# Two attention layers with a dense layer after each: in the second attention stage, a block's averages are moved from the start of the block ahead of it to the middle of the one before that

## The chip, the cores and the metric

The kernel runs on one core of one Trainium2 chip. The metric is the device time of one execution in microseconds (us); the time of a kernel is the median of its runs. Five engines work side by side, each in the order of its own instructions, and wait for each other by semaphores: PE (TensorE, matrix products into PSUM), DVE (VectorE), ACT (ScalarE), POOL (GpSimd) and SP (SyncE, which here issues every DMA).

## The reference

All tensors are float32. There are 2048 rows of 640, 32 heads of 20, and 1536 hidden columns; A and B are applied in turn, twice, each to the row-normalized x and each added to x.

```python
def A(x):                       # linear attention with a learned feature map
    q, k, v = split(x @ wqkv)   # 32 heads of 20
    pq, pk = q @ w_phi, k @ w_phi            # per head
    phi_q = concat(softmax(pq), softmax(-pq))
    phi_k = concat(softmax(pk), softmax(-pk))
    kv, z = phi_k.T @ v, phi_k.sum(rows)     # over all 2048 rows
    o = (phi_q @ kv) / (phi_q @ z + 1e-6)
    return o @ wo
def B(x):                       # dense, Mish, dense
    h = x @ w1 + b1
    return (h * tanh(softplus(h))) @ w2
x = x + A(norm(x)); x = x + B(norm(x)); x = x + A(norm(x)); x = x + B(norm(x))
```

## The kernel before

Each layer has three stages. The first attention stage makes the features of all rows: keys and values go into one PSUM tile that sums `kv` and `z` over all rows, and the queries' features, turned, are spilled to DRAM tensors `e_d`, one for each block. The **second attention stage** (`attend_second`, L783) needs the finished `kv`: it loads the turned features again, multiplies them with `kv`, divides, turns the result, multiplies it with `wo` and adds it to x. The dense stage follows.

The rows are cut into NB = 8 blocks of 256, and a block into two tiles of 128 rows, t = 0 and 1. For each block the second stage has these steps:

- `load(b)` (L755): three DMAs that bring the turned features of block b from `e_d` (two big tiles and one small one).
- `average(b, t)` (L791): 22 small products (L801) of these features with `kvb`, 64 rows at a time, into the two banks of one PSUM tile named `mm`. They give numerators and denominators of the 32 heads. It returns a function that divides.
- `divide` (L808): on DVE, add 1e-6 to the denominators (L816, twice), reciprocal (L817), multiply (L820, twice), into a row tile `xn`.
- `Transposed(rows).all()` (L326): ten PE transpositions of the two divided row tiles, into three PSUM tiles named `one` (four, four and two transpositions). ACT copies the high part of each out (`xth`), and DVE subtracts it for the low part (`xtl`, L332). Products are made from high and low parts, three for each.
- `Rows.half(c, ps)` (L832): fifteen products of 128 x 320 (L416) with `wo` into one `one` tile; then DVE adds them to x (L840) and takes statistics for the next norm (L841). Of the two row tiles `r0` and `r1`, each has two halves: four halves a block, sixty products.

The PSUM tiles named `one` come from a pool of four buffers, those named `mm` from a pool of two; a new tile takes the buffer that was given out longest ago, and its first writer waits until the readers of the old tile have ended. A block takes seven `one` tiles in this order: r0 half 0, r0 half 1, r1 half 0, three for the transpositions, r1 half 1.

Within this stage the order on PE, DVE and SP is the order in which the code is written (`tc.manual_schedule`); ACT and POOL are ordered by a scheduler. `block(b)` (L848) begins with the averages of block b + 1 and their divisions; then come r0's halves, r1's first half, the transpositions of block b + 1, and r1's second half. Behind it stand the mean of r1 (L845), the statistics on POOL (L300, L301), the store of the block (L884), fetches and parts of weights for the dense stage, and the steps of `tail`, which end the features of the last two row tiles of the first stage: softmax sums (L452 to L464), the turn on DVE (L514) and their spills (L518). These are spread over blocks 0 to 3. The loads of block b + 3 are issued in the middle of block b. The averages of blocks 0 and 1 stand ahead of the loop.

Of the kernel before, what the change touches and what calls it, by code (L numbers as in the profile page):

```python
# [24 lines left out]
BT = 2  # L25
BLK = BT * P
NB = S // BLK
# [24 lines left out]
def kernel(  # L52
# [25 lines left out]
    def one_tile():  # L78
        return psum.tile([P, 512], F32, tag="one", name="one", bufs=4)
# [10 lines left out]
    def row_block(t, b):  # L90
        return t[b * BLK:(b + 1) * BLK, :].rearrange("(p t) d -> p t d", t=BT)
# [203 lines left out]
    def norm_scale(b, mvs, t0=0, later=False):  # L295

        n = len(mvs)
        ve = work.tile([P, BT], F32, tag="ve", name="ve", bufs=2)
        for t in range(n):
            nc.gpsimd.tensor_scalar(ve[:, t:t + 1], mvs[t][:, 1:2], LN_EPS, 1.0, op0=ALU.add, op1=ALU.mult)  # L300
        nc.gpsimd.tensor_tensor(stats[:, b, 0, t0:t0 + n], ve[:, :n], neg_half[:, :n], op=ALU.pow)  # L301

        def shifts():
            for t in range(n):
                nc.vector.tensor_scalar(stats[:, b, 1, t0 + t:t0 + t + 1], mvs[t][:, 0:1],
                                        stats[:, b, 0, t0 + t:t0 + t + 1], -1.0, op0=ALU.mult, op1=ALU.mult)
        if later:
            return shifts
        shifts()

    class Transposed:
# [25 lines left out]
        def all(self):  # L337
            while len(self.hs) < KD:
                self.step()
            return self  # L340
# [25 lines left out]
    def row_tile():  # L366
        return work.tile([P, D], F32, tag="xn", name="xn", bufs=4)
# [41 lines left out]
    def project_half(ps, xts, t, ws, col, c, ks=range(KD), w=HC, final=KD - 1, ns=(0, 1, 2), end=2):  # L409
        sl = slice(t * P, (t + 1) * P)  # L410
        cs = slice(col + c * w, col + (c + 1) * w)
        for k in ks:
            h, l, wh, wl = xts.hs[k], xts.ls[k], ws[k][0][:, cs], ws[k][1][:, cs]
            for n in ns:
                a, r = ((h, wh), (h, wl), (l, wh))[n]
                nc.tensor.matmul(ps[:, :w], a[:, sl], r, start=(k == 0 and n == 0),  # L416
                                 stop=(k == final and n == end))

    def halves():
        mm = mm_tile()  # L420
        return [mm[:, 0], mm[:, 1]]
# [46 lines left out]
    def fetch(x_src, b, xt=None):  # L468
        xt = x_tile() if xt is None else xt
        nc.sync.dma_start(xt, row_block(x_src, b))  # L470
        return xt
# [311 lines left out]
    def attend_second(x_src, x_dst, acc, fetches, makes, fetch_next, begin_next):  # L783
        kva, o_ws, loaded, rest, late = acc
        rows = {}
        div = [None]

        def tail(i):
            next(late[i], None)

        def average(b, t, po=None):  # L791

            phs = loaded[b]
            po = halves() if po is None else po
            for g in range(G):
                n = 120 if g < 10 else 80
                w = GW if g < 10 else 42
                c, j = divmod(g, 8)
                for q in range(2):
                    s0 = t * P + 64 * q  # L800
                    nc.tensor.matmul(  # L801
                        po[c][64 * q:64 * q + 64, GW * j:GW * j + w], phs[g][:n, s0:s0 + 64],
                        kvb[:n, g, :w], start=True, stop=True)
            if t == BT - 1:
                del loaded[b]
            return lambda: divide(b, po)

        def divide(b, po):  # L808

            o = row_tile()  # L810
            den = work.tile([P, H], F32, tag="r", name="den", bufs=2)
            pv = [po[c][:, :(DH + 1) * n].rearrange("p (h d) -> p h d", d=DH + 1)
                  for c, n in ((0, 24), (1, 8))]
            hh = (slice(0, 24), slice(24, H))
            for c in range(2):
                nc.vector.tensor_scalar_add(den[:, hh[c]], pv[c][:, :, DH], DEN_EPS)  # L816
            nc.vector.reciprocal(den, den)  # L817
            for c in range(2):
                n = hh[c].stop - hh[c].start
                ins = nc.vector.tensor_tensor(o.rearrange("p (h d) -> p h d", d=DH)[:, hh[c]], pv[c][:, :, :DH],  # L820
                                        den[:, hh[c]].unsqueeze(2).to_broadcast([P, n, DH]), op=ALU.mult)
                div[0] = ins.ins
            rows.setdefault(b, []).append(o)

        class Rows:


            def __init__(self, b, t, cur):
                self.b, self.t, self.xt, self.cur = b, t, xs[b], cur
                self.bn = work.tile([P, 2, 6], F32, tag="bn", name="bn", bufs=2)  # L830

            def half(self, c, ps):  # L832
                if self.b == self.t == c == 0:
                    for ks in ((0, 1), (2, 3), (4,)):
                        for ns in ((0, 1), (2,)):
                            project_half(ps, self.cur, 0, o_ws, 0, 0, ks, ns=ns)
                else:
                    project_half(ps, self.cur, self.t, o_ws, 0, c)
                part = self.xt[:, self.t, c * HC:(c + 1) * HC]
                nc.vector.tensor_tensor(part, ps[:, :HC], part, op=ALU.add)  # L840
                nc.vector.bn_stats(self.bn[:, c], part)  # L841

            def mean(self):
                mv = work.tile([P, 2], F32, tag="mv", name="mv", bufs=3)
                nc.vector.bn_aggr(mv, self.bn)  # L845
                return mv

        def block(b, cur, behind=()):  # L848

            if b == NB - 1:  # L850
                ahead[0].all()
            elif b:
                for t in range(BT):
                    average(b + 1, t)()
            r0, r1 = Rows(b, 0, cur), Rows(b, 1, cur)
            for d in behind[:1]:
                d()
            r0.half(0, one_tile())
            if b:
                tail(0)  # L860
                tail(1)
            for d in behind[1:]:
                d()
            if b + 1 < NB:
                xs[b + 1] = fetch(x_src, b + 1)
            if 0 < b and b + 3 < NB:
                loaded[b + 3] = load(b + 3)
            if b == NB - 3:
                fetch_next()
            r0.half(1, one_tile())  # L870
            mv0 = r0.mean()
            if left:
                left.pop()()
            if b == 1:
                tail(1)
            if b == NB - 2:
                ahead.append(begin_next())
            r1.half(0, one_tile())
            if b + 1 < NB:
                cur = Transposed(rows.pop(b + 1)).all()  # L880
            r1.half(1, one_tile())
            left.append(norm_scale(b, [mv0, r1.mean()], later=True))
            xt = xs.pop(b)
            nc.sync.dma_start(row_block(x_dst, b), xt)  # L884
            makes[b]()
            if b + 1 < NB:
                fetches[b + 1]()
            tail(0)
            for _ in range((0, 1, 1, 2)[b] if b < 4 else 0):
                tail(1)  # L890
            return cur

        ahead, left = [], []
        E = mybir.EngineType
        with tc.manual_schedule(engines={E.PE, E.SP, E.DVE}):
            kv = finish_kv(kva)
            next(rest)
            next(kv)
            xs = {0: fetch(x_src, 0)}
            fetches[0]()  # L900
            next(rest)
            next(kv)
            next(rest)
            tail(0)
            tail(0)
            first = [average(0, t) for t in range(BT)]
            for d in first:
                d()
            with tc.issue_after(div[0]):
                loaded[2] = load(2)  # L910
            tail(0)
            singles = [one_tile(), one_tile()]
            behind = [average(1, 0, singles), average(1, 1)]
            loaded[3] = load(3)
            cur = Transposed(rows.pop(0))
            pair = halves()
            cur.step()
            cur.step(pair[0])
            cur.step(singles[1][:, BLK:])
            for b in range(NB):  # L920
                cur = block(b, cur, () if b else behind)
            left.pop()()
            assert all(next(g, 0) == 0 for g in late)
        return ahead[0]
# [248 lines left out]
```

## Time and profile before

| what | value |
|---|---|
| median of 3 runs | 1355.46 us (1354.35 to 1355.51) |
| the profiled execution | 1355.98 us, of which the span is 1354.1 us |
| granted TensorE clock | 1.0 |
| busy in the span: PE, DVE, ACT, POOL | 1348.3, 1069.7, 584.6, 468.9 us |
| second attention stage, layer 0, averages of block 2 to those of block 7 | 264.71 to 328.86 us |
| the same in layer 1 | 926.08 to 990.23 us |

A row of a timeline gives the start in us from the span's start, the duration in us, the engine, the line, the operation, the tile written and the tiles read, and the shape; x10 are ten that follow each other, whose duration is that from the first start to the last end. In brackets stands how long the engine had been idle, and which engine ended it. PE's products are pipelined: one may start before the one ahead of it has ended. SPq rows are issues of DMAs.

### The profile page before, as it was taken

What the parts mean: (1) busy time and instruction counts of PE and PEld (TensorE: products, weight loads), DVE (VectorE), ACT (ScalarE), POOL (GpSimd) and SP (SyncE); (2) the same over time, 40 slices, a digit from 0 to 9 for tenths busy, and PEclk for the clock granted to TensorE, in tenths of its full rate; (3) what the DMA queues carried; (4) which work ended last, traced back from release to release, by engine and by line L of the source; (5) the groups of instructions that cost most, each with busy time, mean ns of one, the idle gap of its engine ahead of it and who ended that gap; (6) DMA issues with size and microseconds to landing.
All of it is one profiled execution on the core that took longest, in us unless ns stands there. A gap on an engine that the chain in (4) does not pass through costs nothing.

```text
span 1354.1 us, 30937 instructions
## 1 busy us (share of the span) xinstructions
PE 1348.3 (100%) x12890; PEld 1336.8 (99%) x12890; DVE 1069.7 (79%) x1810; ACT 584.6 (43%) x1039; POOL 468.9 (35%) x357
## 2 busy tenths in 40 slices
PE   9999999999999999999999999999999999999999
PEld 9999999999999999999999999999999999999998
DVE  7988888886787888778779888888768776676775
ACT  6344444222554555445444344432236444444443
POOL 3345544444322222122225556744441211111112
PEclk9999999999999999999999999999999999999999
DMA  9623336798613543334573534468964231233200
GB/s 345 176 49 73 79 60 132 195 281 275 207 28 88 118 117 85 54 97 114 147 225 69 114 71 77 81 159 241 286 242 121 79 83 27 88 98 98 66 33 21
DMA packets 350757, 169.21 MB, mean 125 GB/s; under 512 B 287241, under 2 KB 324089, under 8 KB 350617
## 3 DMA queue, kind: packets, MB, share of 16 engines
q1 hardware_dynamic: 350617, 167.23, 46.3%
q8 instruction: 101, 1.65, 0.5%
q14 instruction: 39, 0.32, 0.1%
HBM read 104.61 MB, written 62.59 MB: 123 GB/s over the span
## 4 chain that ended last, share of the span: by engine, by line
PE 99%; DMA 1%; issue 0%; ACT 0%; DVE 0%; POOL 0%; SPq 0%; POOLq 0%
PE mm L416 28%; PE one L941 25%; PE mm L981 24%; PE one L416 13%; PE mm L801 3%; PE one L326 2%; PE one L501 2%; PE mm L273 1%; DMA v<-in_wv 1%; PE one L542 0%; PE mm L999 0%; DMA r1l<-wp_d 0%; PE one L273 0%; PE one L981 0%; PE one L801 0%; PE one L999 0%
## 5 line engine op out<-in xcount | busy, mean ns | idle before, releaser
L967 POOL TENSOR_TENSOR ol<-big,ol 128x512 fp32r<-128x512 f32 (+1 forms) x98 | 130.6, 1332 | 484.7 <-ACT ol L966 400.7
L981 PE MATMUL mm<-r2h,ol 128*128 128x320 f32 x1236 | 295.5, 309 | 0.0
L941 PE MATMUL one<-xtl,r1h 128*128 128x256 f32 x960 | 268.2, 279 | 0.0
L941 PE MATMUL one<-xth,r1l 128*128 128x256 f32 x960 | 268.0, 279 | 0.0
L941 PE MATMUL one<-xth,r1h 128*128 128x256 f32 x960 | 265.9, 279 | 0.0
L981 PEld LDWEIGHTS mm<-r2h,ol 128*128 128x128 f32 x1236 | 211.9, 188 | 0.0
L981 PE MATMUL mm<-r2l,ol 128*128 128x320 f32 x618 | 190.6, 309 | 0.0
L416 PE MATMUL mm<-r1h,xth 128*128 128x304 f32 (+1 forms) x600 | 185.1, 309 | 0.0
L416 PE MATMUL mm<-r1h,xtl 128*128 128x304 f32 (+1 forms) x600 | 183.8, 307 | 0.0
L416 PE MATMUL mm<-r1l,xth 128*128 128x304 f32 (+1 forms) x600 | 183.6, 306 | 0.0
L941 PEld LDWEIGHTS one<-xtl,r1h 128*128 128x128 f32 x960 | 180.4, 188 | 0.0
L941 PEld LDWEIGHTS one<-xth,r1l 128*128 128x128 f32 x960 | 180.4, 188 | 0.0
L941 PEld LDWEIGHTS one<-xth,r1h 128*128 128x128 f32 x960 | 179.6, 188 | 0.0
L956 DVE TENSOR_SCALAR big<-big 128x512 f32<-128x512 f32 (+1 forms) x98 | 56.3, 575 | 111.4 <-ACT big L954 111.2
L465 POOL TENSOR_TENSOR big<-big,r 128x1280 f32<-128x1280 f32 x42 | 101.4, 2419 | 69.3 <-DVE r L464 44.4
L954 ACT ACTIVATE big<-one,b1s 128x256 f32<-128x256 f32 x192 | 80.8, 467 | 91.1 <-PE one L941 90.2
L958 ACT ACTIVATE big<-big,two 128x512 f32<-128x512 f32 (+1 forms) x98 | 70.1, 716 | 115.4 <-DVE big L957 115.4
L966 ACT ACTIVATE ol<-big 128x512 fp32r<-128x512 f32 (+1 forms) x98 | 60.9, 622 | 133.5 <-DVE big L965 133.4
L981 PEld LDWEIGHTS mm<-r2l,ol 128*128 128x128 f32 x618 | 116.1, 188 | 0.0
L416 PEld LDWEIGHTS mm<-r1h,xth 128*128 128x128 f32 x600 | 112.8, 188 | 0.6
L416 PEld LDWEIGHTS mm<-r1h,xtl 128*128 128x128 f32 x600 | 112.8, 188 | 0.4
L416 PEld LDWEIGHTS mm<-r1l,xth 128*128 128x128 f32 x600 | 112.8, 188 | 0.0
(186 smaller groups left out, 3147.3 us busy)
## 6 DMA issues: line engine op xcount, KB each, us to landing
big<-e_d SPq DMA_DIRECT2D x30, 640.0 KB, 6.5
x_d<-xt SPq DMA_DIRECT2D x23, 640.0 KB, 5.1
e_d<-r SPq DMA_DIRECT2D x88, 160.0 KB, 4.0
xt<-x_d SPq DMA_DIRECT2D x22, 640.0 KB, 5.6
n_d<-xn SPq DMA_DIRECT2D x176, 80.0 KB, 2.2
xt<-in_x SPq DMA_DIRECT2D x15, 640.0 KB, 4.3
xn<-x_d SPq DMA_DIRECT2D x28, 320.0 KB, 4.2
v<-n_d SPq DMA_DIRECT2D x30, 256.0 KB, 3.4
```

Source lines behind the costliest of these rows:

```text
L326: nc.tensor.transpose(ps[:, c, t * P:(t + 1) * P], self.rows[t][:, (c0 + c) * P:(c0 + c + 1) * P], ident)
L416: nc.tensor.matmul(ps[:, :w], a[:, sl], r, start=(k == 0 and n == 0), stop=(k == final and n == end))
L465: nc.gpsimd.tensor_tensor(eg, eg, r.unsqueeze(2).to_broadcast([P, 2 * H, DH]), op=ALU.mult)
L501: nc.tensor.matmul(kva[32 * q:32 * q + DH + 1, c:c + 2 * DH], v[:, (DH + 1) * h:(DH + 1) * (h + 1)], e[:, 2 * DH * h:2 * DH * (h + 1)], st ...
L801: nc.tensor.matmul(po[c][64 * q:64 * q + 64, GW * j:GW * j + w], phs[g][:n, s0:s0 + 64], kvb[:n, g, :w], start=True, stop=True)
L941: nc.tensor.matmul(ph[:, j, :], l, r, start=(n == 0), stop=(n == 3 * KD - 1))
L954: exps[0] = nc.scalar.activation(part(ta, 0)[:, j - js.start], ph[:, j, :], AF.Exp, bias=b1s[:, 2 * pr + j:2 * pr + j + 1]).ins
L956: nc.vector.tensor_scalar_min(e, e, E_CAP)
L958: nc.scalar.activation(r, n, AF.Ln, bias=two)
L966: nc.scalar.activation(ah[:, js], n, AF.Copy)
L967: nc.gpsimd.tensor_tensor(al[:, js], n, ah[:, js].bitcast(F32), op=ALU.subtract)
L981: nc.tensor.matmul(ps[:, :HC], l[:, j, t * P:(t + 1) * P], w2s[f][w][:, c * HC:(c + 1) * HC], start=(f == 0 and n == 0), stop=(f == KF - 1 ...
```

## The change

The averages of block b + 2 with their 44 products are written in the middle of block b, behind the ten transpositions of block b + 1 and ahead of the fifteen products of r1's second half; their divisions stand right behind that half. At the start of a block no averages are left. It concerns the averages of blocks 2 to 7, six times a layer.

```diff
             if b == NB - 1:
                 ahead[0].all()
-            elif b:
-                for t in range(BT):
-                    average(b + 1, t)()
             r0, r1 = Rows(b, 0, cur), Rows(b, 1, cur)
...
             r1.half(0, one_tile())
             if b + 1 < NB:
                 cur = Transposed(rows.pop(b + 1)).all()
+            divisions = [average(b + 2, t) for t in range(BT)] if b + 2 < NB else []
             r1.half(1, one_tile())
+            for d in divisions:
+                d()
             left.append(norm_scale(b, [mv0, r1.mean()], later=True))
```

On PE, at the end of block 0 and the start of block 1, before (`r2h` and `r2l` are high and low parts of `wo`; an L416 row is one product; the rows shown are the end of r1's second half, the averages of block 2, and the start of r0's first half of block 1):

```order
L416 MATMUL one<-r2h_3199,xth 128x320
L416 MATMUL one<-r2l_3200,xth 128x320
L416 MATMUL one<-r2h_3199,xtl 128x320
L801 MATMUL mm<-kvb,big 64x63 x20
L801 MATMUL mm<-kvb,ol 64x42 x2
L801 MATMUL mm<-kvb,big 64x63 x20
L801 MATMUL mm<-kvb,ol 64x42 x2
L416 MATMUL one<-r2h_1785,xth 128x320
L416 MATMUL one<-r2l_1786,xth 128x320
```

And now (the end of r1's first half, the transpositions of block 1, the averages of block 2, and the start of r1's second half of block 0):

```order
L416 MATMUL one<-r2l_3200,xth 128x320
L416 MATMUL one<-r2h_3199,xtl 128x320
L326 MATMUL one<-ident,xn 128x128 x10
L801 MATMUL mm<-kvb,big 64x63 x20
L801 MATMUL mm<-kvb,ol 64x42 x2
L801 MATMUL mm<-kvb,big 64x63 x20
L801 MATMUL mm<-kvb,ol 64x42 x2
L416 MATMUL one<-r2h_1785,xth 128x320
L416 MATMUL one<-r2l_1786,xth 128x320
```

The averages have moved ahead by the fifteen products of r1's second half, which now run straight into those of the next block's r0.

On DVE, at the same place, before (L840 and L841 belong to r1's second half of block 0, then its mean, the turn of `tail`, and the first of the two divisions):

```order
L840 TENSOR_TENSOR xt<-one,xt 128x320
L841 BN_STATS bn<-xt 128x6
L845 BN_AGGR mv<-bn 128x2
L514 STREAM_TRANSPOSE r_3156<-r_3156 128x1280
L816 TENSOR_SCALAR den<-mm 128x24
L816 TENSOR_SCALAR den<-mm 128x8
L817 RECIPROCAL den<-den 128x32
```

And now, from the start of the second division to the second add of r0 in block 1:

```order
L816 TENSOR_SCALAR den<-mm 128x24
L816 TENSOR_SCALAR den<-mm 128x8
L817 RECIPROCAL den<-den 128x32
L820 TENSOR_TENSOR xn<-mm,den 128x480
L820 TENSOR_TENSOR xn<-mm,den 128x160
L845 BN_AGGR mv<-bn 128x2
L514 STREAM_TRANSPOSE r_3156<-r_3156 128x1280
L840 TENSOR_TENSOR xt<-one,xt 128x320
L841 BN_STATS bn<-xt 128x6
L452 TENSOR_REDUCE m<-big 128x32 x2
L840 TENSOR_TENSOR xt<-one,xt 128x320
```

Both divisions have moved ahead of the mean and of L514; all of it still stands between r1's last add of one block and r0's first add of the next. ACT, POOL and SP keep their order in the whole program, and so do the stages outside of this one.

## The prediction

> **What bounds the kernel now.** I read the page's first part, then the chain of waits, then the timelines of PE, DVE and SyncE in the second attention stage. All stretches are of the first layer's stage.
>
> ```profile
> PE 1348.3 (100%) x12890; PEld 1336.8 (99%) x12890; DVE 1069.7 (79%) x1810; ACT 584.6 (43%) x1039; POOL 468.9 (35%) x357
> ```
>
> PE is busy for all but 5.8 us of the 1354.1 us span, so nothing that another engine saves shortens the kernel; only PE's own work, or a wait put on PE, moves the end. The chain, read in order of time, says how long one block of the stage takes:
>
> ```profile
> 264.71 2.70 PE mm L801 x88
> ...
> 277.71 2.70 PE mm L801 x88
> ...
> 926.08 2.70 PE mm L801 x88
> ```
>
> From one block's averages (L801) to the next is 13.00 us, all of it PE. The row of the second layer that answers to the first of them (926.08) is as long, and so is what I reckon for each layer. Inside that, PE's timeline shows ten transpositions (L326), the fifteen products of r1's second half (L416), the averages, and so on:
>
> ```profile
> 261.26 1.25 PE L326 MATMUL one<-ident,xn 128*128 128x128 f32 x10
> 262.27 0.40 PE L416 MATMUL one<-r2h,xth 128*128 128x320 f32 x1
> ...
> 264.40 0.31 PE L416 MATMUL one<-r2h,xtl 128*128 128x320 f32 x1
> 264.64 1.38 PE L801 MATMUL mm<-kvb,big 120*64 120x63 f32 x40
> ...
> 274.04 1.25 PE L326 MATMUL one<-ident,xn 128*128 128x128 f32 x10
> 275.24 0.41 PE L416 MATMUL one<-r2h,xth 128*128 128x320 f32 x1
> ...
> 287.05 1.25 PE L326 MATMUL one<-ident,xn 128*128 128x128 f32 x10
> ```
>
> In block 0 the products follow the transpositions' start by 1.01 us, in block 1 by 1.20: PE waits 0.19 there, the one wait of the stage's middle. DVE shows for what:
>
> ```profile
> 264.75 0.49 DVE L840 TENSOR_TENSOR xt<-one,xt 128x320 f32<-128x320 f32 x1 [0.61 <-PE one L416]
> 265.27 0.49 DVE L841 BATCH_NORM_STATS2 bn<-xt 128x6 f32<-128x320 f32 x1
> 265.80 0.21 DVE L845 BATCH_NORM_AGGREGATE mv<-bn 128x2 f32<-128x12 f32 x1
> 265.93 1.46 DVE L514 STREAM_TRANSPOSE r<-r 128x1280 f32<-128x1280 f32 x1
> 267.31 0.22 DVE L816 TENSOR_SCALAR den<-mm 128x24 f32<-128x24 f32 x2
> ...
> 270.23 0.48 DVE L840 TENSOR_TENSOR xt<-one,xt 128x320 f32<-128x320 f32 x1
> ...
> 272.60 0.48 DVE L840 TENSOR_TENSOR xt<-one,xt 128x320 f32<-128x320 f32 x1
> ...
> 274.70 0.48 DVE L840 TENSOR_TENSOR xt<-one,xt 128x320 f32<-128x320 f32 x1
> ...
> 277.75 0.49 DVE L840 TENSOR_TENSOR xt<-one,xt 128x320 f32<-128x320 f32 x1 [0.51 <-PE one L416]
> ...
> 282.85 0.49 DVE L840 TENSOR_TENSOR xt<-one,xt 128x320 f32<-128x320 f32 x1 [0.63 <-PE one L416]
> ...
> 285.76 0.43 DVE L840 TENSOR_TENSOR xt<-one,xt 128x320 f32<-128x320 f32 x1
> ```
>
> The add at 274.70 ends at 275.18 and PE starts at 275.24, 0.06 later: the fifteen products write the PSUM buffer that this add frees. The rule of the four buffers named one: each tile takes the buffer of the one four before it, so the three transposition tiles wait for the adds of the last block's r1 second half, of r0 first half and of r0 second half, in this order. In brackets stands DVE's idle time: it has some at 277.75 and 282.85, but between the adds at 264.75 and 274.70 no row has any. In block 1 DVE is as tight as PE.
>
> **The change, part by part.** No instruction is added or removed; PE's total stays. SP, ACT and POOL issue in the same order.
>
> (a) PE: the averages go in front of r1's second half. Its products start later by the averages' 2.70 us plus the price of entering them from a transposition, which the trace does not show. From L416 it is 0.24 from start to start (264.40 to 264.64), against 0.15 between two L416 (fourteen steps from 262.27 to 264.40). From L326 I bound it so: the transpositions' own step of 0.11 at least, the whole 0.24 at most.
>
> ```profile
> L326 PE MATMUL one<-ident,xn 128*128 128x128 f32 x86 | 11.3, 274 | 0.0
> ```
>
> The step: ten end 1.25 after the first start, one lasts 0.27, so nine steps are 0.98. I take 0.17, the middle: the last transposition starts at 262.24, the averages at 262.41, the products at 265.11 instead of 262.27, 2.84 later. The next block's r0 then follows L416 without a switch. The switch costs 0.09 over the own step before (0.24 less 0.15) and 0.06 now (0.17 less 0.11): PE gains 0.03 a block, 0.2 a layer over six blocks; by the two ends a gain of 0.5 (nothing over the step) or a loss of 0.2.
>
> The Trainium skill ("TensorEngine Tiling (Array Packing)", Tiling Modes, Key Properties) says that changing the tiling mode drains TensorE. It speaks against any gain here: the averages use 64-column tiles, and as many switches remain, one in, one out. The trace agrees that a switch costs, 0.24 against 0.15. With the same 0.09 charged after a transposition the gain would be nothing and the sum 0.4 us higher.
>
> (b) The removed wait: 0.19 in block 1. With averages between the transpositions and those products, the add at 274.70, even 2.84 later, ends at 278.0, and the products start after 278.7. Gone: -0.19 a layer. What is late next is in (c).
>
> (c) DVE: the add of r1's second half waits for products that end 2.84 later, and the two divisions (267.31 to 270.23, 2.92 us) now stand between it and everything of the next block. On DVE behind them are the mean, the turn of L514, and the next block's adds, for which PE's transpositions wait. Since block 1's row of DVE work has no idle time, it moves as one piece: the set between the adds at 264.75 and 272.60 is the same in another order. The add of r0's second half ends at 272.60 + 0.48 + 2.84 = 275.92, and PE may write the third transposition tile at 275.98. PE reaches this tile (the ninth transposition) at 274.04 + 8 x 0.11 = 274.91. **PE waits 1.07 us** where it waited for nothing.
>
> Block 2 then starts 1.07 - 0.19 = 0.88 late. The add of 277.75 comes at 277.75 + 2.84 + 0.88 = 281.47. Behind it: to the mean 1.05 (264.75 to 265.80), divisions 2.92, mean 0.13, from r0's first add to its second 2.91 (282.85 to 285.76, with softmax sums in between), the add 0.43: 7.44, so 288.91, and 288.97 for PE. The ninth transposition is due at 287.05 + 0.88 + 0.87 = 288.80. **PE waits 0.17 us.**
>
> Block 3 has L514 (1.38, 265.93 to 267.31) ahead of its first add but nothing between its two adds, where block 2 has 2.0 us of sums: DVE is some 0.6 us better placed against PE, so about 0.4 us of room is left. Blocks 4 to 6 have neither, 1.8 us of room. Block 7 starts as before.
>
> (d) DMA: the store of a block waits for that late add, so it is issued 2.84 us later, and SyncE's queue behind it (spills, the next rows, the next loads) moves too. The averages need their loads 2.3 us sooner. The loads of block 7 are the ones to watch:
>
> ```profile
> 303.85 0.34 SPq L884 DMA_DIRECT2D x_d<-xt  x1
> ...
> 314.08 0.95 SPq L762 DMA_DIRECT2D big<-e_d  x2
> 315.07 0.52 SPq L763 DMA_DIRECT2D ol<-e_d  x1
> ```
> ```profile
> 328.86 2.70 PE mm L801 x88
> ```
> ```profile
> big<-e_d SPq DMA_DIRECT2D x30, 640.0 KB, 6.5
> ```
>
> The last is issued at 315.07 and lands, by the median of the big ones, 6.5 later, at 321.6; its averages start at 328.86. Now the issue is at 315.07 + 2.84 + 0.9 (PE's lag) = 318.8, the landing at 325.3, and the averages at 328.86 - 2.3 + 0.9 = 327.5. Two us of the seven are left: hidden, cost nothing. If that cover goes, every us of landing beyond it is a us of PE.
>
> **Sum.** A layer: 1.07 + 0.17 - 0.19 - 0.2 = 0.85; two layers 1.7 us. The profiled execution took 1355.98, its span and 1.9 around it, and would take 1357.7. It lies 0.5 above the median of the runs shown, so the median goes from 1355.46 to **1357.2 us**, 0.13% up. With the unknown switch at its ends and the second wait between 0 and 0.4 the sum is 0.8 to 2.9: 1356.3 to 1358.4.
>
> **Rivals.**
> Hidden: PE's waits in (c) do not come, because the add is not what frees that buffer, or DVE makes up time. Against it: the wait at 275.24 obeys the buffer rule to 0.06 us. Then only the gains stay, 0.19 and 0.2 to 0.5 a layer: 1354.1 to 1354.7, say 1354.6.
>
> Slower, by late loads: the averages wait for their own loads in each layer. It decides from a landing over 8.7 us behind the issue instead of 6.5 (for the last load of block 7; block 6 is alike). For it: the DMA queues are full in this stretch and everything in them moves as a train. Against: the move keeps their order and spacing. At 2 us of wait a layer, in addition to the sum, 1361.2.
>
> Slower, by a tighter DVE: the room of 0.4 in block 3 is used up too and the switch costs its upper end: 1.07 + 0.4 + 0.3 - 0.19 + 0.2 = 1.8 a layer, 1359.0.
>
> That the change does nothing of what it says is excluded by the order of instructions.
>
> **How the numbers follow.** Forecast 0.60, hidden 0.10, late loads 0.15, tighter DVE 0.13; 0.02 for a gain I cannot name (the gains above end at 1.4 us). A measurement of this kernel can tell about 0.2% from no change, that is 1352.7 to 1358.2. The forecast's range lies within it but for its upper tip (0.04 of chance), hidden lies in it, both slower cases beyond it. So faster 0.02, same 0.66, slower 0.32. The range 1354.5 to 1360.2 covers the hidden case, the forecast's own range, the tighter DVE and the nearer part of the late loads; the worst loads and the nameless gain, about 0.1, are left out.
>
> **What would show it.** Right: in the changed profile PE's ninth transposition of block 1 stands about 1.1 us behind the eighth, with DVE's second add of r0 just before it, and that of block 2 some 0.2; the products behind block 1's averages start without a wait; no average waits for a DMA; blocks 4 to 6 take some 12.76 us. Wrong: transpositions without a break (hidden), a wait of L801 for e_d, a break in block 3, or DVE gaps between the adds of block 1.

## The result, and the profile after

| | us |
|---|---|
| before, median of 14 runs | 1355.45 (1354.35 to 1356.11) |
| after, median of 14 runs | 1357.59 (1356.21 to 1359.59) |
| after against before | ratio 1.0017, 95% interval 1.001 to 1.0024 |
| forecast | 1357.2, range 1354.5 to 1360.2 |

The change makes the kernel 2.1 us slower, 0.16% by the medians (the table's ratio says 0.17%). That is clear of no change, and inside the 0.2% that the prediction called the same, though the interval reaches to 0.24%; the forecast was 1.7. The profiled execution of after took 1359.59, 2.0 above its median; where these 2 us lie is shown at the end of this section.

The first part of the page, after, and its chain of waits by engine:

```profile
PE 1349.3 (99%) x12890; PEld 1337.9 (99%) x12890; DVE 1065.1 (78%) x1810; ACT 585.5 (43%) x1039; POOL 468.9 (35%) x357
...
PE 98%; DVE 1%; DMA 0%; issue 0%; SPq 0%
```

PE still is the whole chain but for one per cent, and DVE, busy for 78% of the span, now holds that one. Where that is, the list of PE's waits says (engine, buffer, line, what it waited for; us in total, times, longest):

```profile
PE mm L801 <- issue: 1.7, 1, 1.7
PE one L326 <- DVE xt L840: 1.6, 2, 0.8
```

The second row is new: PE's transpositions wait for the adds of L840, once a layer. The chain in order of time (start, us, what) shows the place in the first layer, block by block:

```profile
262.40 2.70 PE mm L801 x88
...
267.54 0.50 DVE xt L840
...
275.33 0.41 DVE xt L840
...
275.79 0.44 PE one L326 x2
276.23 2.70 PE mm L801 x88
...
289.13 2.70 PE mm L801 x88
...
301.92 2.70 PE mm L801 x88
...
314.70 2.70 PE mm L801 x88
...
327.49 2.70 PE mm L801 x88
```

Read the starts of the averages (L801): 13.83 us from block 2's to block 3's, then 12.90, 12.79, 12.78, 12.79. Between 267.5 and 275.7 the chain leaves PE for DVE: the first row of DVE is the add of r1's second half, the last the second add of r0, and left out between them are the divisions, the turn of L514, r0's first add and the two softmax maxima of L452. PE's own timeline at the two places:

```profile
261.15 1.25 PE L326 MATMUL one<-ident,xn 128*128 128x128 f32 x10
262.33 1.39 PE L801 MATMUL mm<-kvb,big 120*64 120x63 f32 x40
...
273.94 1.03 PE L326 MATMUL one<-ident,xn 128*128 128x128 f32 x8
275.79 0.44 PE L326 MATMUL one<-ident,xn 128*128 128x128 f32 x2 [0.82 <-DVE xt L840]
...
287.76 1.37 PE L326 MATMUL one<-ident,xn 128*128 128x128 f32 x10
...
300.67 1.25 PE L326 MATMUL one<-ident,xn 128*128 128x128 f32 x10
```

The row of ten has become eight and two. The ninth starts at 275.79; eight steps of 0.11 behind 273.94 it was due at 274.81, so the break is 0.98 (the 0.82 in brackets counts from the end of the eighth's row, which is longer than its step). In block 2 the ten take 1.37 instead of 1.25: 0.12 of wait. DVE, beside it:

```profile
267.54 0.49 DVE L840 TENSOR_TENSOR xt<-one,xt 128x320 f32<-128x320 f32 x1 [3.50 <-PE one L416]
...
275.25 0.48 DVE L840 TENSOR_TENSOR xt<-one,xt 128x320 f32<-128x320 f32 x1
...
300.54 0.47 DVE L840 TENSOR_TENSOR xt<-one,xt 128x320 f32<-128x320 f32 x1
```

The add at 275.25 ends at 275.73 and PE goes on at 275.79, the 0.06 of before. Note the bracket of the first row: DVE stands idle for 3.50 us in front of the late add, and is the late one for the 7.7 us behind its end (268.03 to 275.73). SyncE's queue, the last load of block 7:

```profile
319.24 1.56 SPq L763 DMA_DIRECT2D ol<-e_d  x1
```

The profile names no wait of the averages for a load.

**The 2 us above the median.** The second layer has the same break, and something of its own, the row "issue" above. It stands in both kernels where the averages of block 1 run, ahead of the stage's loop; before:

```profile
913.15 0.68 PE L801 MATMUL mm<-kvb,xt 120*64 120x63 f32 x16 [0.76 <-issue]
```

After, and then the granted clock in three stretches behind it (third number from the end of a row, ahead of the DMA share and GB/s):

```profile
914.64 0.68 PE L801 MATMUL mm<-kvb,xt 120*64 120x63 f32 x16 [1.73 <-issue]
```
```profile
915.00:916.10 1.10, 1.10 (x38) 1.05 (x33) 0.26 (x1) 0.00 (x0) 0.69 (x1) 1.00 0.95 297
916.20:919.40 3.20, 3.20 (x16) 3.20 (x15) 1.66 (x4) 1.47 (x3) 1.57 (x1) 0.50 0.88 284
919.60:925.00 5.40, 5.40 (x39) 5.40 (x39) 4.74 (x14) 0.00 (x0) 0.17 (x1) 1.00 0.43 155
```

PE stops for 1.73 us, goes on at the full clock, and from 916.1 to 919.5 it gets half of it. Whether that belongs to the change is one of the questions below.

### The profile page after: what moved, and what is told of

The parts are those of the page before. It is cut to its first block, busy times and chain, and to the rows that moved or that the text cites. A ratio compares the mean times of both kernels' runs of the same rounds, so it can differ in the third digit from the quotient of the medians.

```text
span 1357.8 us, 30937 instructions
## 1 busy us (share of the span) xinstructions
PE 1349.3 (99%) x12890; PEld 1337.9 (99%) x12890; DVE 1065.1 (78%) x1810; ACT 585.5 (43%) x1039; POOL 468.9 (35%) x357
## 4 chain that ended last, share of the span: by engine, by line
PE 98%; DVE 1%; DMA 0%; issue 0%; SPq 0%
PE mm L416 28%; PE one L941 25%; PE mm L981 24%; PE one L416 12%; PE mm L801 3%; PE one L326 2%; PE one L501 2%; PE mm L273 1%; PE mm L999 0%; DMA raw<-in_wqk_t 0%; PE one L273 0%; PE one L981 0%; DVE m L452 0%; DVE r L514 0%; DVE xt L840 0%
## 5 line engine op out<-in xcount | busy, mean ns | idle before, releaser
L416 PE MATMUL mm<-r1h,xth 128*128 128x304 f32 (+1 forms) x600 | 185.1, 308 | 0.0
L416 PE MATMUL mm<-r1h,xtl 128*128 128x304 f32 (+1 forms) x600 | 183.8, 307 | 0.0
L416 PE MATMUL mm<-r1l,xth 128*128 128x304 f32 (+1 forms) x600 | 183.6, 306 | 0.0
L416 PEld LDWEIGHTS mm<-r1h,xth 128*128 128x128 f32 x600 | 112.8, 188 | 0.6
L416 PEld LDWEIGHTS mm<-r1h,xtl 128*128 128x128 f32 x600 | 112.7, 188 | 0.4
L416 PEld LDWEIGHTS mm<-r1l,xth 128*128 128x128 f32 x600 | 112.8, 188 | 0.0
```

## The experiments

The theory: PE loses by the DVE work that stands between the last add of one block's r1 and the second add of the next block's r0, because the third transposition tile takes the buffer that this add frees. The rivals: the new place of the averages costs by itself (on PE, by the switch of tile shapes, or by stores and loads that are issued later); or the loss is not in blocks 0 to 2.

One measure serves all kernels, from the chain rows of the first layer: the time from the start of block 2's averages to that of block 7's, five blocks. Before it is 328.86 - 264.71 = 64.15, after 327.49 - 262.40 = 65.09: 0.94 more a layer, 1.88 in two. The second layer's five blocks take the same to 0.02 us in every kernel.

**1. Both divisions ahead of the late add.** PE's order is that of the changed kernel, DVE does the divisions in front of r1's second half, as before.

```diff
             divisions = [average(b + 2, t) for t in range(BT)] if b + 2 < NB else []
-            r1.half(1, one_tile())
             for d in divisions:
                 d()
+            r1.half(1, one_tile())
```

> The changed kernel with one thing moved: the two divisions stand ahead of r1's second half in the order of DVE, right behind the averages. Theory (the price is the divisions' 2.92 us on DVE ahead of the next block's adds): DVE has 3.50 us without work between its low parts and r1's last add, so the divisions fit there, PE's breaks between the eighth and ninth transposition of blocks 1 and 2 (1.09 and 0.12 us) go, the wait of 0.19 in block 1 stays away, and the time falls 0.4 to 0.9 us under the kernel before, to about 1354.8. Rival (averages in the middle cost PE by themselves, by switches or late loads): the time stays near the changed kernel's 1357.6.

Measured: 1355.25 us against 1355.71, ratio 0.9997 (0.9988 to 1.0006). PE's transpositions of block 1, and the averages behind them:

```profile
274.63 1.25 PE L326 MATMUL one<-ident,xn 128*128 128x128 f32 x10
275.81 1.39 PE L801 MATMUL mm<-kvb,big 120*64 120x63 f32 x40
```
```profile
263.10 2.70 PE mm L801 x88
...
327.03 2.70 PE mm L801 x88
```

The ten are one row again, and the five blocks take 63.93. The whole loss is gone though PE's order and the late store are the changed kernel's. So the place of the averages costs nothing; the place of the divisions does. The 63.93 is 0.22 below before: the old wait of block 1, and no more. That is 0.44 in two layers, the lower end of what was expected, and the medians, 0.46 apart, can't tell it from nothing.

**2. One division ahead, one behind.** This is the dose between the two.

```diff
-            r1.half(1, one_tile())
-            for d in divisions:
+            for d in divisions[:1]:
+                d()
+            r1.half(1, one_tile())
+            for d in divisions[1:]:
                 d()
```

> As the changed kernel, but the first of the two divisions stands ahead of the adds of r1's second half, the second behind them. Theory (PE loses by the DVE time that stands between r1's last add and the second add of r0): one division is 1.46 us, the break in block 1 was 0.98 and that in block 2 0.12 us, so both go and some 0.4 us of room is left; the time is that of the kernel with both divisions ahead, 1355.3 us, and the transpositions run without a break. Rival (the averages in front of the products cost by themselves, on PE or by late stores and loads): 1357.5, the break smaller or not. Rival (the cost is in proportion to what stands there): half the loss, 1356.5.

Measured: 1354.56 us against 1355.59, ratio 0.9994 (0.9986 to 1.0003). DVE's add of r0's second half in block 1, PE's row of transpositions there, and the chain:

```profile
273.70 0.48 DVE L840 TENSOR_TENSOR xt<-one,xt 128x320 f32<-128x320 f32 x1
```
```profile
273.86 1.25 PE L326 MATMUL one<-ident,xn 128*128 128x128 f32 x10
```
```profile
262.33 2.70 PE mm L801 x88
...
326.26 2.70 PE mm L801 x88
```

The add ends at 274.18 and PE may write at 274.24; the ninth transposition is due at 273.86 + 0.87 = 274.73. There are 0.49 us of room, as expected, and again 63.93 for the five blocks. A division of 1.46 us taken away removes the whole wait of 0.98, not 1.46 and not half: this is a race with a threshold.

**3. A filler behind the divisions.** A maximum over 960 columns, which nothing reads, stands on DVE behind each pair; the outputs stay the same.

```diff
             for d in divisions:
                 d()
+            if divisions:
+                fill = work.tile([P, 1], F32, tag="fill", name="fill", bufs=2)
+                nc.vector.tensor_reduce(fill, xs[b].rearrange("p t d -> p (t d)")[:, :960], axis=AX.X, op=ALU.max)
```

> The changed kernel with one more DVE instruction behind each pair of divisions, a maximum over 960 columns of x that nobody reads, some 1.1 us long. Theory: it adds to what stands ahead of the next block's adds, so PE's break grows to about 2.2 us in block 1, 1.2 in block 2 and 0.6 in block 3, and blocks 4 to 6, with 1.8 us of room, show none; 2.8 us a layer over the changed kernel, 7.8 us over the kernel before, about 1363.2. Rival (the breaks come from something else than DVE's queue): the filler falls into DVE's idle time and the time stays near 1357.6.

Measured: 1362.93 us against 1355.71, ratio 1.0051 (1.0038 to 1.0065). The filler's row and PE's breaks:

```profile
271.37 1.14 DVE L884 TENSOR_REDUCE fill<-xt 128x1 f32<-128x960 f32 x1
```
```profile
276.81 0.44 PE L326 MATMUL one<-ident,xn 128*128 128x128 f32 x2 [1.72 <-DVE xt L840]
...
290.76 0.44 PE L326 MATMUL one<-ident,xn 128*128 128x128 f32 x2 [0.96 <-DVE xt L840]
...
304.19 0.44 PE L326 MATMUL one<-ident,xn 128*128 128x128 f32 x2 [0.26 <-DVE xt L840]
```
```profile
262.36 2.70 PE mm L801 x88
...
330.20 2.70 PE mm L801 x88
```

Where the changed kernel's brackets hold 0.82, then no entry, then none, there are 1.72, 0.96 and 0.26: block 1 gained 0.90 (its row of eight is 0.17 longer too, 0.1 of it a wait of the fifth transposition), block 2 its full wait, and block 3's room of half a microsecond has turned into one. The five blocks take 67.84. (Behind them, in block 7, the products after the transpositions wait 0.18 for an add, the kind of wait that experiment 5 is about.) By the starts of the averages, blocks 1 and 2 take 1.05 and 1.06 more than in the changed kernel for the filler's 1.14 us: past the threshold DVE's time goes over to PE nearly one to one.

**4. The change for the averages of blocks 4 to 7 alone.** Those of blocks 2 and 3 keep the old place.

```diff
+            elif 0 < b < 3:
+                for t in range(BT):
+                    average(b + 1, t)()
...
-            divisions = [average(b + 2, t) for t in range(BT)] if b + 2 < NB else []
+            divisions = [average(b + 2, t) for t in range(BT)] if 1 < b < NB - 2 else []
```

> The change for the averages of blocks 4 to 7 alone; those of blocks 2 and 3 stand where they stood before. Theory (all of the price is in blocks 1 and 2, where the first stage's last softmax fills DVE): no break of PE in any block but the old 0.19 in block 1, time within 0.4 us of the kernel before, 1355.1 to 1355.6. Rival (each moved average costs a little, by the switch or by its loads): two thirds of the change's loss, about 1356.9.

Measured: 1355.72 us against 1355.71, ratio 1.0 (0.9991 to 1.0008). The chain:

```profile
264.00 2.70 PE mm L801 x88
...
277.00 2.70 PE mm L801 x88
...
287.58 2.70 PE mm L801 x88
...
325.95 2.70 PE mm L801 x88
```

From 264.00 to 325.95 are 61.95; at the seam the averages come earlier by the fifteen products, a row of 2.20, and 64.15 with these is what before takes. The old 13.00 of block 1 is there, the later blocks neither gain nor lose. Late loads, which would have shown here, are excluded, as they are by the changed kernel's own list of waits.

**5. The change for blocks 2 and 3 alone.** The other half; the averages of blocks 4 to 7 keep the old place.

```diff
+            elif b > 2:
+                for t in range(BT):
+                    average(b + 1, t)()
...
-            divisions = [average(b + 2, t) for t in range(BT)] if b + 2 < NB else []
+            divisions = [average(b + 2, t) for t in range(BT)] if b < 2 else []
```

> The change for the averages of blocks 2 and 3 alone; those of blocks 4 to 7 stand where they stood before. Theory: all of the loss, about 1.0 us a layer: breaks of 1.1 and 0.1 us in blocks 1 and 2, about 1357.5. Rival (each moved average costs a little): a third of the loss, about 1356.1.

Measured: 1359.48 us against 1355.71, ratio 1.0027 (1.0016 to 1.0037). That is a miss: 3.8 us lost where the whole change loses 2.1. PE's waits and its timeline say why:

```profile
PE one L416 <- DVE xt L840: 1.9, 2, 0.9
PE one L326 <- DVE xt L840: 1.6, 2, 0.8
```
```profile
275.70 0.44 PE L326 MATMUL one<-ident,xn 128*128 128x128 f32 x2 [0.82 <-DVE xt L840]
...
287.67 1.37 PE L326 MATMUL one<-ident,xn 128*128 128x128 f32 x10
289.97 0.42 PE L416 MATMUL one<-r2h,xth 128*128 128x320 f32 x1 [0.93 <-DVE xt L840]
```
```profile
289.43 0.48 DVE L840 TENSOR_TENSOR xt<-one,xt 128x320 f32<-128x320 f32 x1
```

The break of block 1 is as in the changed kernel. In block 2, where the seam leaves no averages between the transpositions and the products of r1's second half, these products wait too: for the buffer that the add of r1's first half frees at 289.91. It is the same buffer rule and the same late DVE; in the changed kernel the 2.70 us of averages cover this wait. Counted from when the products were due (287.67 + 1.01 + 0.12 = 288.80) they wait 1.17, and twice that is all but 0.1 of the 2.4 us by which the two layers' five blocks exceed the changed kernel's. I had counted the wait that the change makes and not the one that it hides. This explanation is tested next.

**6. The same two blocks, with the divisions ahead.**

```diff
-            r1.half(1, one_tile())
             for d in divisions:
                 d()
+            r1.half(1, one_tile())
```

> As the kernel with the change for the averages of blocks 2 and 3 alone, but with the divisions ahead of the adds of r1's second half. That kernel took 1359.5 and its trace has, besides the breaks of the transpositions in block 1, a wait of 0.93 us a layer in front of r1's second half in block 2, where no averages stand between the transpositions and these products any more. Theory (this wait too is the divisions' time on DVE, passed on because the 2.7 us of averages are not there to cover it): DVE had 1.47 us of idle time ahead of the late add in block 2 and 3.5 in block 1, which the divisions now use; both waits go, 1355.5 us. Rival (the seam between the two orders costs by itself, by the missing averages alone): the break in block 1 goes, the 0.93 stays, 1357.4. Rival (all of the excess is something outside of this): 1359.

Measured: 1355.46 us against 1355.59, ratio 1.0 (0.9991 to 1.0008).

```profile
262.87 2.70 PE mm L801 x88
...
287.35 1.09 PE one L326 x10
288.44 2.20 PE one L416 x15
...
329.00 2.70 PE mm L801 x88
```

Products follow transpositions without a wait in block 2, although no averages stand between. From 262.87 to 329.00 are 66.13, less the 2.20 of the seam 63.93. Both waits were the divisions' time.

**7. The changed kernel once more, on the chip of 2 and 6.**

> The changed kernel once more, on the same chip as the two others and beside the kernel before. Theory: 1357.3 to 1357.6 us, 1.7 to 2.1 above before; the break of the transpositions 1.0 us in block 1 and 0.1 in block 2 of both layers. The stretch ahead of the second layer's loop, where the first profile showed a longer issue stall and a slower granted clock, tells whether that belongs to the change: if it does, the stall is 1.7 us again, if not, it is about the 0.8 of before.

Measured: 1357.27 us against 1355.59, ratio 1.0015 (1.0006 to 1.0024).

```profile
PE one L326 <- DVE xt L840: 1.6, 2, 0.8
```
```profile
262.50 2.70 PE mm L801 x88
...
327.59 2.70 PE mm L801 x88
```

The breaks are the same and the five blocks take 65.09 again. The stall ahead of the second layer's loop is not there at all: no row of PE's waits names "issue". It isn't the change's. The profiled execution of 2 and that of 4 have none either; 0.57 stood in that of 1, 1.01 in 3, 0.46 in 5 and 0.86 in 6.

| kernel | five blocks, us | twice the difference to before | medians, after less before |
|---|---|---|---|
| before | 64.15 | | |
| the change | 65.09 | +1.88 | +2.14, again +1.68 |
| 1, divisions ahead | 63.93 | -0.44 | -0.46 |
| 2, one ahead | 63.93 | -0.44 | -1.03 |
| 3, filler | 67.84 | +7.38 | +7.22 |
| 4, blocks 4 to 7 | 64.15 | 0 | +0.01 |
| 5, blocks 2 and 3 | 66.29 | +4.28 | +3.77 |
| 6, these with divisions ahead | 63.93 | -0.44 | -0.13 |

The five blocks account for every median to about 0.6 us. Stops like the one above, of another length in each profiled execution, are large enough for the rest, but that they make it is not shown. Kernels 1 and 2 show no loss and in their traces 0.44 us less over the five blocks of both layers, but their intervals hold 1: no version here is shown to beat before.

## Why the prediction was right, step by step

- **(a), the averages ahead of r1's second half**: the order cost nothing, as its sum nearly said, but the gain of 0.2 a layer isn't there. From the start of the ten transpositions (261.15) to the averages (262.33) are 1.18; nine steps are 0.98, so the switch is 0.20, not the 0.17 taken: 0.09 over the own step of 0.11, as it is 0.09 over the 0.15 of the products. Blocks without a wait take 12.78 to 12.79 in both kernels, not 12.76. The Trainium skill's statement ("TensorEngine Tiling (Array Packing)", Tiling Modes, Key Properties) that a change of mode drains TensorE, weighed there against the gain, fits: as many switches, 0.09 each. No row shows the drain itself.
- **(b), the old wait**: right. The products behind block 1's averages follow without a wait, and the kernels without a break are 0.22 shorter over five blocks, where the wait was put at 0.19.
- **(c), DVE**: right in mechanism, place and nearly in size. The ninth transposition of block 1 waits 0.98 (forecast 1.07) for r0's second add, to the 0.06 us of the buffer rule. The term most off is the piece of DVE work that the prediction took over at its old length: from the late add to r0's second add it takes 7.71 (267.54 to 275.25) in its new order, before 7.85 (264.75 to 272.60). Block 2: 0.12 (0.17). Block 3: the add ends at 301.01, the ninth transposition is due at 300.67 + 0.87 = 301.54, so about 0.5 of room (0.4). In blocks 4 to 6 even kernel 3's 1.14 us brought no break of the transpositions (room forecast 1.8). Kernels 1, 2 and 3 show that the divisions' time is the cause, by taking away all of it, half of it, and adding to it.
- **(d), DMA**: right. The last load went out at 319.24 (318.8), block 7's averages started at 327.49 (327.5), and no average waited for a load. The load landed 6.8 behind its issue, at 326.0, so 1.5 us of cover were left where the prediction had 2.2. The later store cost nothing (kernel 1 has it too).
- **The sum**: 0.94 a layer in the trace against 0.85: 0.98 and 0.12 for the breaks, 0.05 more until PE is in step again (block 1 takes 1.04 over 12.79), less 0.21 for the old wait. The errors went both ways: the breaks were forecast 0.14 too large, the switch's gain 0.2 too large, and the 0.05 were missing. The 0.4 us that the prediction added for a switch without gain give 2.1, which is what the medians show; that these agree to a tenth is luck, since medians of this kernel move by half a microsecond.

Of the rivals, "hidden" fell with the break, "late loads" with the list of waits and kernel 4, and the tighter DVE with block 3's room. The last was nearer than its price tells: kernel 3's 1.14 us were enough to bring it.

## What to carry to other kernels

An engine that is idle for a fifth of the time can still set the pace in a stretch: look for its rows without idle time in brackets, and count from the end of such a stretch back to the last event that another engine gave it. Work that an in-order queue can do while it waits for a late producer belongs in front of that wait (here 2.9 us into 3.5 us of idle time), behind it the same work is on the path. When a change puts work between a release and its use, count the waits that this work hides as well as those it makes: take the work out again, as a half-done change does, and they come back.

## What the runs showed of the hardware that I had not expected

- Five of the eight profiled executions above, and that of before, show PE stopped with no releaser in the profile, for 0.46 to 1.73 us, at the same instruction: the fifth product of a tile in the averages of block 1 in the second layer. It comes and goes between executions of one kernel (1.73 and none for the changed one). The DMA share from 912 to 918 us hardly tells them apart: 1.04 and 1.03 in kernels 2 and 7, without a stop, and 1.01 in kernel 6, with one of 0.86. One thing in the kept traces does go with it. The queue that the profile calls "instruction" (q8) moves packets of 16 KB, and in all six executions its last packet ahead of PE's restart ends 1.36 to 1.58 us before the restart (after: 913.06 and 914.64; before: 911.73 and 913.15), however long the stop. In the three without a stop, the same product starts 1.11 to 1.46 behind such an end. That fits a wait for PE's own instructions; no run tests it, and the cause stays open.
- After the longest of these stops the granted clock fell to 0.50 for some 3.4 us, from 916.1 to 919.5, though PE had been going again since 914.64; in the 3.4 us ahead of the fall it was busy for 1.67. After the stop of 0.76 in before the clock stayed at 1.00. From the transpositions behind the stop to block 2's averages this execution takes 10.61 us (915.93 to 926.54), that of kernel 7, the same program, 9.44 (914.32 to 923.76). The two spans differ by 2.8 (1357.8 and 1355.0): the stop and this slow stretch, 1.73 and 1.17, nearly make that up.
